# A place table made anew for a fused attention and feed-forward kernel

## The chip, the cores and the metric

The kernel runs on one core of one Trainium2 chip. The metric is the device time of one execution in microseconds; of several executions the median counts. The five engines of the core run side by side, each through its own list of instructions in a fixed order: TensorE (PE, with weight loads shown as PEld), VectorE (DVE), ScalarE (ACT), GpSimd (POOL) and SyncE (SP, which issues nearly all DMA transfers here). They meet only at semaphores.

## The reference

```python
q_n, k_n, c_n = (t / (norm(t) + 1e-06) for t in (q, k, centroids))     # q, k, v: 4 x 8 x 768 x 64
q_assign = argmax(q_n @ c_n.T); k_assign = argmax(k_n @ c_n.T)           # one of 16 clusters
mask = q_assign[..., :, None] == k_assign[..., None, :]
scores = where(mask, q @ k.T / sqrt(64), -1e9)
attn = exp(scores - max(scores)); attn = attn / (sum(attn) + 1e-9)
x = (attn @ v).transpose(0, 2, 1, 3).reshape(3072, 512)
h = x @ w_in                                                              # 512 x 2048
g = h * tanh(softplus(h))
out = g @ w_out                                                           # 2048 x 512
```

## The kernel before

There are 32 heads (4 batches of 8). A head's 768 query rows make three units of 256 rows, 96 units in all, and each unit has two halves of 128 rows. A half goes through: `scores` (four fp32 matrix products, lines 622 and 627, the second pair adding the cluster mask), `rowmax` (DVE, line 637), `expo` (ACT, line 651), a reciprocal of the row sums, `p_hi` and `p_lo` (lines 695 and 706, the split of the weights into two fp16 parts), a transposing DMA (line 736), and `pv` (lines 778 and 785). The first 24 units, the heads of batch 0, go another way: fp32 transposes on PE (`turn`, line 712), copies back on ACT (`back_t`, line 728) and fp32 products (line 759).

When a batch's heads are done, its feed-forward part begins, in 24 blocks of 256 rows by 256 columns of the hidden layer for each batch: `m1` (lines 856 to 858), `e_mish` (ACT, line 866), `e_gh` (POOL, line 870), `e_gl` (DVE, line 878), `m2` (lines 897 to 899), `m_out` and `m_store`. So `m1` and `m2` of one batch lie between the attention of the next.

Ahead of this stand preparations. Every weight tile is loaded as 64-bit words (`w_load`) and turned into fp32 by `w_abs` (ACT, line 262), `w_f32` and `w_or` (DVE, lines 270 and 277). Every head's operands A, B, T and Z are made from the loaded q and k (`prep_sc`, `prep_hi`, `prep_lo`, lines 444 to 461) and by copies between halves of the partitions (`copy_t`, `copy_z`, `copy_a`, `copy_b`, lines 467 to 473; a DMA for the most part, an ACT or DVE copy for some heads). `hot_copy` puts the rows with the cluster marks into Z and T by four small DMAs (lines 612 and 613). `warm` is a group of eight small matmuls without use for the result (line 289).

Each such step is a function, and the table `PLAN` gives every call of every function a place, 0 to 3682. The steps are issued in the order of their places, and so each engine's list is the order of places cut down to that engine's instructions:

```python
    def run(self):
        for op in sorted(self.ops, key=lambda op: self.ops[op][0]):
            self.issue(op)
```

The scores lie in PSUM buffers with the tag S, of which there are two; a buffer is free again when the exponential (`expo`) that reads it is done. So a half's scores can start only when the exponential of an earlier half has run. The blocks of `m1` have two PSUM buffers as well (tag H), freed by `e_mish`. All DMAs here stand in SP's one list, where an instruction that waits holds up all behind it.

Of the kernel before, what the change touches and what calls it, by code (L numbers as in the profile page):

```python
# [971 lines left out]
def spread(*axes):  # L972
    return list(itertools.product(*axes))


def places(args, text):
# [5 lines left out]
        0 1 2 3 4 5 6 15 18 19 20 67 68 69 92 93 94 95 96 97 116 117 240 241  # L982
# [20 lines left out]
        13 29 124 102 242 400 614 531 798 714 926 1116 1148 1276 1500 1360 1723 1727 1867 1792 2024 2090 2190 2314 2487  # L1003
        2426 2576 2716 2881 2963 3005 3131
    """),
    'assign_mm': places(spread((0, 1)), """
        14 55
    """),
    'prep_sc': places(spread(range(0, 32)), """
        16 56 158 215 454 602 675 818 899 715 1130 1246 1149 1322 1521 1361 1724 1728 1868 1793 2161 2091 2191 2315 2488  # L1010
        2427 2577 2717 2882 2964 3006 3132
    """),
    'prep_hi': places(spread(range(0, 32)), """
        17 57 194 342 455 603 676 819 900 1028 1131 1247 1336 1437 1575 1655 1775 1869 2016 2067 2177 2273 2376 2492
        2570 2670 2784 2878 3021 3090 3185 3276
    """),
    'w_load': places(spread(range(0, 32)), """
        22 21 26 37 28 40 31 134 44 51 112 135 132 173 161 235 80 98 47 36 146 175 238 298 234 255 299 319 330 340 387
        420
    """),  # L1020
    'w_abs': places(spread(range(0, 32)), """
        23 25 27 62 30 99 41 166 74 119 144 216 176 217 219 272 125 126 159 160 182 237 305 327 316 317 359 360 410 411
        439 472
    """),
    'w_f32': places(spread(range(0, 32)), """
        24 81 65 88 48 100 72 178 108 120 163 232 230 254 253 293 147 127 226 294 208 257 306 350 334 336 395 375 461
        418 440 473
    """),
    'v_load': places(spread(range(0, 4), range(0, 4)), """
        45 32 34 35 225 452 156 655 1084 1157 1546 1502 1900 1981 2332 2365  # L1030
    """),
    'copy_t': places(spread(range(0, 32)), """
        33 59 195 358 456 632 741 822 973 1045 1132 1260 1337 1438 1576 1656 1776 1883 2017 2070 2197 2276 2441 2512
        2600 2696 2785 2895 3024 3091 3186 3292
    """),
    'prep_lo': places(spread(range(0, 32)), """
        38 58 213 372 457 604 677 820 924 1029 1158 1248 1369 1457 1584 1665 1782 1870 2019 2068 2178 2274 2431 2493
        2571 2671 2827 2893 3022 3107 3196 3277
    """),
    'copy_a': places(spread(range(0, 32)), """  # L1040
        39 60 271 437 567 636 779 887 1025 1064 1159 1283 1370 1501 1585 1722 1848 1948 2061 2110 2198 2284 2442 2565
        2601 2743 2836 2977 3077 3155 3250 3375
    """),
    'assign_hot': places(spread((0, 1)), """
        42 66
    """),
    'assign_first': places(spread((0, 1)), """
        43 75
    """),
    'w_or': places(spread(range(0, 32)), """  # L1050
        46 82 79 89 49 101 150 218 109 121 169 286 288 263 278 333 148 145 227 296 209 258 307 351 335 341 396 409 462
        419 441 500
    """),
    'assign_put': places(spread((0, 1)), """
        50 76
    """),
    'copy_z': places(spread(range(0, 32)), """
        52 83 214 373 545 624 678 821 925 1044 1173 1249 1390 1458 1600 1666 1790 1886 2049 2069 2208 2275 2458 2494
        2649 2730 2828 2894 3030 3108 3227 3291
    """),  # L1060
    'rows_z': places(spread((0, 1)), """
        53 84
    """),
    'rows_t': places(spread((0, 1)), """
        54 85
    """),
    'hot_copy': places(spread(range(0, 32)), """
        61 86 262 450 592 633 742 895 1030 1046 1174 1261 1391 1459 1601 1670 1791 1887 2050 2071 2236 2277 2459 2513
        2650 2731 2889 2896 3031 3109 3228 3293
    """),  # L1070
    'copy_b': places(spread(range(0, 32)), """
        63 162 279 436 546 649 780 823 974 1047 1229 1321 1456 1517 1664 1743 1812 1936 2055 2094 2209 2327 2476 2529
        2659 2751 2862 2929 3034 3122 3262 3301
    """),
    'scores': places(spread(range(0, 96), (0, 1)), """
# [9 lines left out]
    """),  # L1085
    'rowmax': places(spread(range(0, 96), (0, 1)), """
# [9 lines left out]
    """),  # L1096
    'expo': places(spread(range(0, 96), (0, 1)), """
# [9 lines left out]
    """),  # L1107
    'turn': places(spread(range(0, 24), (0, 1), (0, 1)), """
# [4 lines left out]
    """),  # L1113
    'back_t': places(spread(range(0, 24), (0, 1), (0, 1)), """
# [4 lines left out]
    """),  # L1119
    'v_sq': places(spread(range(0, 4), range(0, 4)), """  # L1120
        103 104 105 106 528 896 613 811 1123 1237 1603 1696 1937 2095 2353 2555
# [237 lines left out]
```

## Time and profile before

| | us |
|---|---|
| three runs | 886.0, 886.37, 889.4 |
| median | 886.37 |
| profiled execution, its own time | 885.66 |
| span in its trace, first to last instruction | 883.9 |
| PE busy in the span | 850.3 |
| ACT busy | 659.3 |
| DVE busy | 614.4 |
| POOL busy | 235.3 |

The profiled execution took 885.66 us, 1.8 us more than its span, and lies 0.7 us below the median of the runs. TensorE had a granted clock of 0.96 in the first 40 us and of 1.00 from there on. Busy time is the union of the engine's instructions; PE's instructions overlap in the record, so that busy PE time holds the small stalls between matmuls too.

### The profile page before, as it was taken

What the parts mean: (1) busy time and instruction counts of PE and PEld (TensorE: products, weight loads), DVE (VectorE), ACT (ScalarE), POOL (GpSimd) and SP (SyncE); (2) the same over time, 40 slices, a digit from 0 to 9 for tenths busy, and PEclk for the clock granted to TensorE, in tenths of its full rate; (3) what the DMA queues carried; (4) which work ended last, traced back from release to release, by engine and by line L of the source; (5) the groups of instructions that cost most, each with busy time, mean ns of one, the idle gap of its engine ahead of it and who ended that gap; (6) DMA issues with size and microseconds to landing.
All of it is one profiled execution on the core that took longest, in us unless ns stands there. A gap on an engine that the chain in (4) does not pass through costs nothing. (4 is left out here: it accounts for less than half of the span.)

```text
span 883.9 us, 16511 instructions
## 1 busy us (share of the span) xinstructions
PE 850.3 (96%) x6271; PEld 608.5 (69%) x6271; DVE 614.4 (70%) x1080; ACT 659.3 (75%) x1058; POOL 235.3 (27%) x371
## 2 busy tenths in 40 slices
PE   7789999999999999999999999999999999999998
PEld 6667676687676676777676765777765765867673
DVE  8999889977767678967867778777767676311120
ACT  5778688899897999789998998788987896411120
POOL 2203454322313323212222413331321312311110
PEclk9999999999999999999999999999999999999999
DMA  9977332467669687977668588966577668300000
GB/s 341 327 231 215 82 105 57 108 122 145 126 118 172 107 175 156 175 149 152 127 110 172 120 162 161 156 126 129 114 129 155 121 124 143 70 13 13 13 13 24
DMA packets 252542, 116.19 MB, mean 131 GB/s; under 512 B 230640, under 2 KB 232816, under 8 KB 252464
## 3 DMA queue, kind: packets, MB, share of 16 engines
q1 hardware_dynamic: 252320, 115.02, 59.8%
q8 instruction: 49, 0.80, 0.4%
q14 instruction: 29, 0.24, 0.1%
q10 hardware_dynamic: 144, 0.13, 0.0%
HBM read 35.68 MB, written 6.29 MB: 47 GB/s over the span
## 5 line engine op out<-in xcount | busy, mean ns | idle before, releaser
L856 PE MATMUL h<-x,w 128*128 128x256 f16 x768 | 209.8, 273 | 3.4 <-ACT u L866 3.1
L651 ACT ACTIVATE p<-s,m 128x768 f32<-128x768 f32 x192 | 172.8, 901 | 52.0 <-DVE m L637 34.3
L858 PE MATMUL h<-x,w 128*128 128x256 f16 x768 | 209.3, 273 | 0.0
L857 PE MATMUL h<-x,w 128*128 128x256 f16 x768 | 209.3, 273 | 0.0
L637 DVE TENSOR_REDUCE m<-s 128x1 f32<-128x768 f32 x192 | 180.7, 948 | 24.2 <-PE s L627 23.4
L706 DVE SCALAR_TENSOR_TENSOR hl<-p,l,hl 128x768 f16<-128x768 f32 x142 | 147.2, 1041 | 61.5 <-ACT hl L695 58.6
L897 PE MATMUL O<-w,g 128*128 128x512 f16 x384 | 146.1, 381 | 0.1
L899 PE MATMUL O<-w,g 128*128 128x512 f16 x384 | 145.5, 379 | 0.0
L898 PE MATMUL O<-w,g 128*128 128x512 f16 x384 | 145.5, 379 | 0.0
L695 ACT ACTIVATE hl<-p,l 128x768 f16<-128x768 f32 x142 | 130.2, 929 | 18.0 <-ACT p L651 9.2
L878 DVE SCALAR_TENSOR_TENSOR g<-u,mscg,g 128x512 f16<-128x512 f32 x96 | 73.6, 777 | 87.9 <-POOL g L870 87.6
L622 PE MATMUL s<-A,B 128*128 128x384 f32 x384 | 117.5, 387 | 14.8 <-ACT p L651 10.7
L870 POOL TENSOR_SCALAR g<-u,mscg 128x512 f16<-128x512 f32 x96 | 70.5, 739 | 221.3 <-ACT u L866 186.1
L866 ACT ACTIVATE u<-h,msch 128x512 f32<-128x512 f32 x96 | 64.0, 685 | 66.2 <-PE h L858 49.0
L92 ACT ACT_TABLE_LOAD x78 | 100.1, 1283 | 2.1 <-PEq L1349 0.7
L627 PE MATMUL s<-Z,T 80*128 80x384 f32 x384 | 99.5, 340 | 0.0
L856 PEld LDWEIGHTS <-w 128*128 128x128 f16 x768 | 75.1, 98 | 21.1 <-issue 10.3
L622 PEld LDWEIGHTS s<-A,B 128*128 128x128 f32 x384 | 62.0, 190 | 39.3 <-ACT p L651 24.3
L663 POOL TENSOR_SCALAR l<-l 128x1 f32<-128x1 f32 x90 | 25.1, 279 | 233.4 <-ACT p L651 231.6
L857 PEld LDWEIGHTS <-w 128*128 128x128 f16 x768 | 75.2, 98 | 14.8 <-issue 4.1
L858 PEld LDWEIGHTS <-w 128*128 128x128 f16 x768 | 75.1, 98 | 8.7
L627 PEld LDWEIGHTS s<-Z,T 80*128 80x128 f32 x384 | 70.2, 190 | 0.0
(204 smaller groups left out, 1120.0 us busy)
## 6 DMA issues: line engine op xcount, KB each, us to landing
qk<-in_qk_dram SPq DMA_DIRECT2D x32, 384.0 KB, 4.0
stage<-in_w_in_dram SPq DMA_DIRECT2D x16, 512.0 KB, 7.6
stage<-in_w_out_dram SPq DMA_DIRECT2D x16, 512.0 KB, 4.5
vraw<-in_vP_dram SPq DMA_DIRECT2D x16, 384.0 KB, 4.5
out_dram<-osb SPq DMA_DIRECT2D x23, 256.0 KB, 2.7
A<-A SPq DMA_DIRECT2D x27, 192.0 KB, 3.1
Z<-B SPq DMA_DIRECT2D x18, 192.0 KB, 3.5
B<-T SPq DMA_DIRECT2D x18, 192.0 KB, 3.3
```

What stands on the lines that cost most here:

```text
L622: nc.tensor.matmul(s[:, j, :384], st["B", n][:, q0 : q0 + P], st["A", n][:, j * 384 : (j + 1) * 384], start=True, stop=False,)
L627: nc.tensor.matmul(s[:, j, :384], st["T", n][: D + NCL, q0 : q0 + P], st["Z", n][: D + NCL, j * 384 : (j + 1) * 384], start=False, stop=True,)
L637: nc.vector.tensor_reduce(m, st["s", i, a][:, :, :384], axis=AX.XY, op=ALU.max, negate=True)
L651: nc.scalar.activation(p.rearrange("p (n x) -> p n x", n=2), st["s", i, a][:, :, :384], AF.Exp, bias=st["m", i, a], scale=1.0, accum_out=l,)
L695: nc.scalar.activation(t[:, 0], p, AF.Copy, scale=r)
L706: nc.vector.scalar_tensor_tensor(t[:, 1], p, r, t[:, 0], op0=ALU.mult, op1=ALU.subtract)
L856: nc.tensor.matmul(o, wh, xh, start=(c == 0), stop=False)
L857: nc.tensor.matmul(o, wh, xl, start=False, stop=False)
L858: nc.tensor.matmul(o, wl, xh, start=False, stop=(c == 3))
L897: nc.tensor.matmul(o, gh, wh, start=(f == 0 and fi == 0), stop=False)
L898: nc.tensor.matmul(o, gh, wl, start=False, stop=False)
L899: nc.tensor.matmul(o, gl, wh, start=False, stop=(f == 7 and fi == 1))
```

## The change

Only the numbers in `PLAN` differ. The program's functions, the constants in `T` and the number of instructions on each engine are the same (PE 6001, DVE 1080, ACT 855, POOL 366 and SP 438 calls of instructions in both). The table was made by a planner that now counts with other durations of the first transfers and of the scores.

```diff
     'warm': places(spread(range(0, 24)), """
-        0 1 2 3 4 5 6 15 18 19 20 67 68 69 92 93 94 95 96 97 116 117 240 241
+        0 1 2 3 4 5 6 17 18 19 20 51 52 116 117 118 119 120 121 122 123 124 131 291
```

The order of units, blocks and heads is by and large the old one. What moves is mostly the neighbourhood: which of two steps of one engine goes first.

Place one, DVE in the first microseconds, from the step behind the centroids on. w are weight tiles (L270 is `w_f32`, L277 `w_or`), B, Z and T operands of heads 0 and 1, D, Dm and onehot the cluster assignment of a head, m0_0 the row maximum of unit 0. In the kernel before:

```order
37 L270 TENSOR_SCALAR w1_292<-w1_292 128x512
38 L461 SCALAR_TENSOR_TENSOR B_0_320<-qk0_244,scq_151,A_0_261 128x768
39 L559 TENSOR_REDUCE Dm0_328<-as0_246 128x12
...
44 L277 SCALAR_TENSOR_TENSOR w1_292<-stage0_289,w1_292 128x512
45 L270 TENSOR_SCALAR w3_304<-w3_304 128x512
46 L277 SCALAR_TENSOR_TENSOR w3_304<-stage4_300,w3_304 128x512
47 L469 CAST Z_0_349<-B_0_320 64x768
48 L590 CAST Z_0_349<-oh0_343 16x3x128 x2
49 L469 CAST B_0_320<-T_0_310 64x768
50 L270 TENSOR_SCALAR w2_298<-w2_298 128x512
51 L559 TENSOR_REDUCE Dm1_379<-as1_355 128x12
53 L637 TENSOR_REDUCE m0_0_406<-s0_0_372 128x1
```

And in the changed kernel:

```order
37 L461 SCALAR_TENSOR_TENSOR B_0_282<-qk0_244,scq_151,A_0_246 128x768
38 L270 TENSOR_SCALAR w1_287<-w1_287 128x512
39 L277 SCALAR_TENSOR_TENSOR w1_287<-stage0_284,w1_287 128x512
40 L469 CAST Z_0_291<-B_0_282 64x768
41 L270 TENSOR_SCALAR w1_287<-w1_287 128x512
42 L559 TENSOR_REDUCE Dm0_314<-as0_306 128x12
...
48 L270 TENSOR_SCALAR w3_303<-w3_303 128x512
49 L277 SCALAR_TENSOR_TENSOR w3_303<-stage4_301,w3_303 128x512
50 L277 SCALAR_TENSOR_TENSOR w1_287<-stage1_294,w1_287 128x512
51 L590 CAST Z_0_291<-oh0_361 16x3x128 x2
52 L469 CAST B_0_282<-T_0_248 64x768
53 L559 TENSOR_REDUCE Dm1_394<-as1_375 128x12
55 L637 TENSOR_REDUCE m0_0_404<-s0_0_388 128x1
```

Head 0's assignment (L559) now comes behind four more instructions, and two more weight steps (the second L270 and L277 on stage 1) stand ahead of the first row maximum. On PE the four `warm` groups that stood behind the assignment's matmuls now stand ahead of them.

Place two, ACT between the exponentials (L651) of units 41 and 42. hl are the fp16 weights of `p_hi` (L695), xf outputs of `pv` (L800), u the Mish of a block (L866). Before:

```order
357 L453 ACTIVATE A_15_4104<-qk15_3217,scq_151 128x768
358 L471 CAST T_15_4106<-A_15_4104 64x768
359 L471 CAST B_14_3873<-T_14_3858 64x768
360 L800 ACTIVATE xf1_2_2_4144<-o19_4114 64x256
361 L651 ACTIVATE p41_1_4162,l41_1_4163<-s41_1_4095,m41_1_4150 128x768
362 L92 ACT_TABLE_LOAD
363 L866 ACTIVATE u19_4192<-h19_4167,msch0_1342 128x512
```

And in the changed kernel:

```order
357 L453 ACTIVATE A_15_4051<-qk15_3258,scq_151 128x768
358 L471 CAST T_15_4053<-A_15_4051 64x768
359 L471 CAST B_14_3866<-T_14_3852 64x768
360 L800 ACTIVATE xf1_2_2_4148<-o19_4123 64x256
361 L800 ACTIVATE xf1_2_0_3979<-o19_4123 64x256
362 L695 ACTIVATE hl40_1_4154<-p40_1_4044,l40_1_4045 128x768
363 L651 ACTIVATE p41_1_4156,l41_1_4157<-s41_1_4110,m41_1_4150 128x768
364 L92 ACT_TABLE_LOAD
```

The exponential of unit 41, second half, now stands behind one more L800 and behind the L695 of unit 40, second half, which stood ahead of L453 before. On PE, at the same place, a group of six `m2` matmuls (block 13 of g, half 1) that stood ahead of the scores of unit 42 now stands behind them.

Place three, SP at the cluster rows of head 20 (Z_20 and T_20), which the scores of unit 60 read. pt are transposes of the fp16 weights hl. Before:

```order
263 L736 DMA_TRANSPOSE pt57_5831<-hl57_0_5780 128x12x128
264 L612 DMA Z_20_5777<-stg20_5868 16x384
265 L613 DMA T_20_5724<-stg20_5868 16x384
266 L612 DMA Z_20_5777<-stg20_5868 16x384
267 L613 DMA T_20_5724<-stg20_5868 16x384
268 L736 DMA_TRANSPOSE pt57_5831<-hl57_1_5890 128x12x128
```

And in the changed kernel:

```order
263 L736 DMA_TRANSPOSE pt57_5822<-hl57_0_5776 128x12x128
264 L736 DMA_TRANSPOSE pt57_5822<-hl57_1_5884 128x12x128
265 L612 DMA Z_20_5769<-stg20_5958 16x384
266 L613 DMA T_20_5736<-stg20_5958 16x384
267 L612 DMA Z_20_5769<-stg20_5958 16x384
268 L613 DMA T_20_5736<-stg20_5958 16x384
```

The four small copies have moved behind the transposing DMA of unit 57, second half. Beside these places, on ACT the exponential of unit 38, second half, has moved ahead of the preparation of head 14's A and T. On PE the step that stands just ahead of a half's four score matmuls is another one in many places. Among the 137 halves from unit 28 on these are, before and now: `m1` 40 and 55, `m2` 38 and 34, other scores 32 and 29, all others (`pv`, assignment, a transpose of the value scale) 27 and 19.

## Rows read from the trace of the kernel before

**Rows 1.** The page's first lines: the span, and PE's busy time, share and instructions.

```profile
span 883.9 us, 16511 instructions
PE 850.3 (96%) x6271; PEld 608.5 (69%) x6271; DVE 614.4 (70%) x1080; ACT 659.3 (75%) x1058; POOL 235.3 (27%) x371
```

**Rows 2.** Busy time of each engine in stretches of the span (start:end, length, then busy us and instructions of PE, PEld, DVE, ACT and POOL, the granted clock, the DMA share and GB/s).

```profile
20.00:90.00 70.00, 60.58 (x568) 47.73 (x567) 67.93 (x132) 53.61 (x113) 15.18 (x15) 0.99 0.81 261
90.00:180.00 90.00, 84.13 (x638) 62.55 (x634) 80.94 (x135) 74.13 (x158) 41.80 (x46) 1.00 0.36 87
180.00:760.00 580.00, 571.36 (x4111) 405.19 (x4109) 429.58 (x731) 501.67 (x743) 153.44 (x258) 1.00 0.72 140
760.00:884.00 124.00, 119.79 (x820) 79.31 (x818) 20.22 (x27) 20.16 (x31) 18.77 (x27) 1.00 0.06 19
```

**Rows 3.** What PE waited for between 180 and 760 us: us in total, times, longest.

```profile
PE s L622 <- ACT p L651: 4.5, 7, 1.2
PE h L856 <- ACT u L866: 3.1, 3, 1.6
PE vs3p L208 <- DVE vs3m L201: 0.3, 1, 0.3
```

**Rows 4.** What DVE waited for between 88 and 196 us, the first line: us in total, times, longest.

```profile
DVE m L637 <- PE s L627: 4.4, 7, 1.1
```

**Rows 5.** DVE's instructions in order of time, 8 to 21 us (start, length, instruction; in brackets idle time before it and what ended it).

```profile
8.57 0.28 DVE L196 COPY C<-ct 64x128 f32<-64x128 f32 x1
8.78 0.41 DVE L270 TENSOR_SCALAR w<-w 128x512 uint32<-128x512 uint32 x1
9.11 1.00 DVE L461 SCALAR_TENSOR_TENSOR B<-qk,scq,A 128x768 fp32r<-128x768 f32 x1
10.55 0.36 DVE L559 TENSOR_REDUCE Dm<-as 128x12 f32<-128x192 f32 x1 [0.44 <-PE as L545]
...
12.39 0.69 DVE L277 SCALAR_TENSOR_TENSOR w<-stage,w 128x512 uint32<-128x512 uint32 x1
...
14.16 0.56 DVE L469 CAST Z<-B 64x768 fp32r<-64x768 f32 x1
14.74 1.12 DVE L590 CAST Z<-oh 16x384 fp32r<-16x384 bf16 x2
15.89 0.93 DVE L469 CAST B<-T 64x768 fp32r<-64x768 f32 x1
16.85 1.94 DVE L270 TENSOR_SCALAR w<-w 128x512 uint32<-128x512 uint32 x1
...
19.48 0.95 DVE L637 TENSOR_REDUCE m<-s 128x1 f32<-128x768 f32 x1
```

**Rows 6.** PE in order of time in the same stretch: the assignment's matmuls, 32 matmuls of four `warm` groups, and the first scores.

```profile
8.91 1.60 PE L545 MATMUL as<-C,qk 128*128 128x128 f32 x12 [0.68 <-DVE C L196]
10.35 1.95 PE L289 MATMUL gram<-identb 128*128 128x128 bf16 x32
...
16.97 0.58 PE L622 MATMUL s<-A,B 128*128 128x384 f32 x2 [2.69 <-DVE B L469]
17.39 0.51 PE L627 MATMUL s<-Z,T 80*128 80x384 f32 x2
```

**Rows 7.** POOL in order of time, 14 to 19 us: the preparation of head 1.

```profile
14.37 1.12 POOL L444 TENSOR_SCALAR qk<-qk,scq 128x768 f32<-128x768 f32 x1 [8.92 <-PE as L545]
15.58 0.83 POOL L451 TENSOR_SCALAR A<-qk 128x768 fp32r<-128x768 f32 x1
16.49 2.01 POOL L459 TENSOR_TENSOR B<-qk,A 128x768 fp32r<-128x768 f32 x1
```

**Rows 8.** PE in order of time at three halves' scores: behind `m1` (line 858), behind `m2` (line 899), and behind other scores.

```profile
666.77 0.59 PE L622 MATMUL s<-A,B 128*128 128x384 f32 x2
667.20 0.51 PE L627 MATMUL s<-Z,T 80*128 80x384 f32 x2
...
465.87 0.70 PE L622 MATMUL s<-A,B 128*128 128x384 f32 x2
466.40 0.52 PE L627 MATMUL s<-Z,T 80*128 80x384 f32 x2
...
311.81 0.52 PE L622 MATMUL s<-A,B 128*128 128x384 f32 x2
312.16 0.52 PE L627 MATMUL s<-Z,T 80*128 80x384 f32 x2
```

**Rows 9.** PE in order of time: the scores of unit 40, first half, with their wait.

```profile
289.35 0.61 PE L622 MATMUL s<-A,B 128*128 128x384 f32 x2 [0.25 <-ACT p L651]
```

**Rows 10.** ACT in order of time, 304 to 311 us: the work ahead of the exponential of unit 41, second half (309.76).

```profile
305.04 1.76 ACT L695 ACTIVATE hl<-p,l 128x768 f16<-128x768 f32 x2 [0.56 <-ACT p L651]
...
309.36 0.38 ACT L800 ACTIVATE xf<-o 64x256 f32<-64x256 f32 x1
309.76 0.90 ACT L651 ACTIVATE p<-s,m 128x768 f32<-128x768 f32 x1
```

**Rows 11.** PE in order of time, 307 to 309 us: the first and the last of a group of six `m2` matmuls, and the `m1` matmul behind them.

```profile
307.19 0.39 PE L897 MATMUL O<-w,g 128*128 128x512 f16 x1
...
308.28 0.38 PE L899 MATMUL O<-w,g 128*128 128x512 f16 x1
...
308.82 0.27 PE L856 MATMUL h<-x,w 128*128 128x256 f16 x1
```

**Rows 12.** The instructions of lines 270 and 277 on DVE: shortest, median and longest in ns, first and last start.

```profile
L270 DVE TENSOR_SCALAR w<-w x32: 384/419/1935, 8.8 to 81.3; 128x512 uint32<-128x512 uint32 x32
L277 DVE SCALAR_TENSOR_TENSOR w<-stage,w x32: 661/692/1280, 12.4 to 85.2; 128x512 uint32<-128x512 uint32 x32
```

**Rows 13.** SP in order of time, 443 to 448 us: the first of the four copies of head 20's cluster rows, the last, and the transposing DMA of unit 57, second half.

```profile
443.26 0.90 SPq L612 DMA_DIRECT2D Z<-stg  x1
...
445.47 0.59 SPq L613 DMA_DIRECT2D T<-stg  x1
447.67 1.44 SPq L736 DMA_TRANSPOSE pt<-hl  x1
```

**Rows 14.** PE in order of time: the scores of unit 60, first half; and of the DMAs by line in 430 to 460 us the copies of cluster rows (KB each, median us from issue to landing).

```profile
455.00 0.70 PE L622 MATMUL s<-A,B 128*128 128x384 f32 x2
...
Z<-stg SPq DMA_DIRECT2D x4, 24.0 KB, 2.1
```

**Rows 15.** What SP waited for in the whole span, the first line: us in total, times, longest.

```profile
SPq L736 <- DVE hl L706: 116.1, 49, 7.7
```

More of the change, by code (lines that the diff above doesn't have):

```diff
@@ L1002 @@
     'qk_load': places(spread(range(0, 32)), """
-        13 29 124 102 242 400 614 531 798 714 926 1116 1148 1276 1500 1360 1723 1727 1867 1792 2024 2090 2190 2314 2487
-        2426 2576 2716 2881 2963 3005 3131
+        13 38 93 125 241 374 594 474 807 679 909 1050 1162 1264 1495 1388 1712 1723 1885 1815 2018 2119 2178 2316 2488
+        2424 2586 2714 2862 2942 2990 3122
+    """),
+    'prep_sc': places(spread(range(0, 32)), """
+        14 62 195 333 441 573 675 812 900 680 1079 1247 1163 1293 1518 1389 1713 1724 1886 1816 2180 2120 2179 2317 2489
+        2425 2587 2715 2863 2943 2991 3123
@@ new lines @@
+    """),
+    'prep_hi': places(spread(range(0, 32)), """
+        15 63 196 334 442 574 676 813 901 1033 1132 1248 1336 1442 1577 1644 1773 1860 2012 2068 2181 2274 2426 2490
+        2567 2673 2773 2883 3015 3104 3185 3284
+    """),
+    'copy_t': places(spread(range(0, 32)), """
+        16 81 228 335 445 598 739 815 977 1048 1133 1258 1337 1443 1578 1645 1774 1862 2013 2071 2198 2277 2435 2502
+        2604 2722 2774 2897 3020 3107 3186 3287
+    """),
+    'prep_lo': places(spread(range(0, 32)), """
+        21 64 203 369 454 575 677 814 924 1046 1155 1249 1372 1451 1586 1664 1778 1861 2027 2069 2182 2275 2431 2491
+        2568 2674 2828 2895 3016 3105 3194 3285
@@ new lines @@
+    """),
+    'w_load': places(spread(range(0, 32)), """
+        22 28 30 39 32 59 40 140 44 75 136 213 174 152 198 248 58 60 141 114 166 156 249 297 231 258 298 312 313 330 373
+        393
+    """),
+    'w_abs': places(spread(range(0, 32)), """
+        23 29 31 50 33 97 69 172 94 111 137 214 204 205 201 301 107 108 167 233 189 240 303 327 292 311 354 355 401 402
+        430 461
+    """),
+    'w_f32': places(spread(range(0, 32)), """
+        24 34 42 74 46 98 89 173 95 112 157 242 229 283 212 302 129 109 238 288 210 259 304 357 336 344 379 366 447 416
+        431 462
@@ new lines @@
+    """),
+    'w_or': places(spread(range(0, 32)), """
+        25 48 78 84 47 99 138 230 96 113 158 279 281 284 286 328 146 150 239 299 211 260 305 358 337 345 380 406 448 417
+        432 491
+    """),
+    'copy_z': places(spread(range(0, 32)), """
+        26 77 227 370 565 597 678 817 925 1047 1165 1257 1386 1452 1594 1665 1800 1889 2050 2070 2203 2276 2447 2492
+        2652 2721 2842 2896 3033 3106 3228 3286
+    """),
+    'copy_a': places(spread(range(0, 32)), """
+        27 115 289 436 490 610 751 816 1013 1074 1156 1288 1373 1522 1587 1717 1838 1942 2045 2094 2199 2328 2436 2571
+        2606 2738 2835 2968 3079 3157 3276 3376
@@ L1005 @@
     """),
     'assign_mm': places(spread((0, 1)), """
[L1007 removed]
+        35 61
     """),
[L1009 to L1011 removed]
+    'assign_hot': places(spread((0, 1)), """
+        36 67
     """),
[L1013 to L1015 removed]
@@ L1016 @@
[L1016 to L1027, printed above, removed]
+    'assign_first': places(spread((0, 1)), """
+        37 76
@@ L1028 @@
     """),
     'v_load': places(spread(range(0, 4), range(0, 4)), """
-        45 32 34 35 225 452 156 655 1084 1157 1546 1502 1900 1981 2332 2365
+        41 49 43 45 215 649 489 656 1123 1129 1530 1394 1896 1996 2359 2365
     """),
[L1032 to L1052, printed above, removed]
+    'w_sq': places(spread(range(0, 32)), """
+        53 90 91 155 224 225 226 275 276 277 278 280 282 285 287 342 383 384 385 386 387 388 389 390 391 392 469 470 502
+        503 518 579
@@ L1122 @@
     """),
     'v_sum': places(spread(range(0, 4)), """
-        107 897 1717 2556
+        106 895 1720 2558
     """),
     'v_turn': places(spread(range(0, 4)), """
-        110 954 1718 2557
+        134 961 1721 2559
     """),
     'v_top': places(spread(range(0, 4)), """
-        111 955 1719 2558
+        135 962 1722 2560
     """),
-    'p_hi': places(spread(range(0, 96), (0, 1)), """
[9 rows of a table removed]
+    'pair_mm': places(spread(range(2, 31, 2)), """
+        151 440 668 897 1113 1308 1559 1758 1918 2154 2372 2551 2768 2978 3170
@@ L1191 @@
-    """),
-    'p_lo': places(spread(range(0, 96), (0, 1)), """
[9 rows of a table removed]
[9 rows of a table added]
     """),
     'invert_pair': places(spread(range(0, 12)), """
-        203 339 427 547 611 605 744 842 915 990 1052 1119
+        190 329 425 543 606 643 746 837 914 995 1058 1115
+    """),
+    'pair_first': places(spread(range(2, 31, 2)), """
+        199 457 674 926 1149 1347 1584 1776 1950 2195 2409 2553 2788 2984 3172
     """),
     'pv': places(spread(range(0, 48), range(0, 3)), """
[7 rows of a table removed]
-    """),
-    'pair_first': places(spread(range(2, 31, 2)), """
-        205 470 674 929 1150 1346 1577 1778 1952 2188 2380 2580 2786 2986 3176
[7 rows of a table added]
@@ L1217 @@
     """),
     'pair_turn': places(spread(range(2, 31, 2)), """
-        206 538 739 930 1151 1347 1578 1779 1953 2189 2389 2581 2787 3028 3198
+        209 534 737 927 1150 1348 1585 1777 1951 2196 2410 2611 2789 3031 3202
     """),
     'v_split': places(spread(range(0, 4), range(0, 4)), """
-        370 368 467 239 1002 1015 1034 1067 1834 1894 1876 1855 2695 2651 2869 2760
+        253 449 648 371 998 1011 1036 1065 1832 1887 1871 1845 2685 2643 2879 2766
+    """),
+    'v_low': places(spread(range(0, 4), range(0, 4)), """
+        254 505 860 496 999 1012 1037 1066 1833 1888 1872 1853 2750 2688 2880 2848
@@ L1223 @@
+    """),
+    'pv_scale': places(spread(range(0, 96)), """
[5 rows of a table added]
     """),
     'pair_put': places(spread(range(2, 31, 2)), """
-        261 539 740 978 1172 1348 1599 1781 2048 2235 2421 2603 2863 3029 3226
-    """),
-    'pv_scale': places(spread(range(0, 96)), """
[5 rows of a table removed]
+        267 535 738 989 1173 1349 1610 1799 2049 2259 2432 2648 2860 3032 3227
     """),
     'pv_out': places(spread(range(0, 96)), """
[5 rows of a table removed]
[5 rows of a table added]
+    """),
+    'w_sum': places(spread((0, 1)), """
+        343 580
     """),
     'x_out': places(spread(range(0, 96)), """
[5 rows of a table removed]
[5 rows of a table added]
```

67 lines of the change are left out of this document (27 added, 40 removed), and 280 rows, old and new, of the table PLAN.

## The prediction

> **What bounds the kernel now.** I read the page's first lines, then the windows, then the waits, and only then single stretches. The page gives PE 96% of the span and DVE 70% [rows 1]; that is a mean over two unlike parts, which the windows take apart [rows 2]. From 20 to 90 us DVE is busy 67.93 of 70 us and PE 60.58: DVE sets the pace, since beside the attention of batch 0 it turns the weights into fp32. From 90 to 180 us DVE has still 80.94 of 90. From 180 to 760 us PE has 571.36 of 580, and from 760 to the end 119.79 of 124. So up to about 180 us a microsecond of DVE is a microsecond of the kernel, and behind it one of PE is. A new order can win what the bounding engine now waits. PE's waits in the long part come to 4.5 us on exponentials, 3.1 us on the Mish and 0.3 us on the value scale, 7.9 us together [rows 3]; the bigger idle sums of ACT, POOL and SP cost nothing by themselves. DVE's largest wait around the first part's end is 4.4 us for scores, in seven pieces [rows 4]. That is what a new table has to work with: some 12 us of 884. What it can lose has no such limit.
>
> **The sum** is made against the profiled execution, 885.66 us (a span of 883.9 and 1.8 around it); the median of the runs, 886.37, is 0.7 above it, and I add that at the end.
>
> **1. The start, on DVE.** Before, the centroids' last copy ends at 8.85 us (8.57 + 0.28), DVE loses 0.44 waiting for the assignment's matmuls, and the first row maximum ends at 20.43 (19.48 + 0.95) [rows 5]. Now PE does the four warm groups first (1.95, of which 0.68 fits in its wait for C), then the assignment (1.60) [rows 6]: 8.91 − 0.68 + 1.95 + 1.60 ≈ 11.8. DVE has from 8.85 on B (1.00), L270 (0.42), L277 (0.69), the Z copy (0.56) and another L270 (0.42), together to 11.94, so the 0.44 goes. Five assignment instructions take 1.93 as before (10.55 to 12.48 in start and end): 13.87. Two L270 and two L277, 2 × 0.42 + 2 × 0.69: 16.1. The one-hot casts (1.12): 17.2. Next is the copy of B out of T. In the kernel before, the L270 that met POOL's third preparation step (16.49, 2.01 long, end 18.50 [rows 7]) took 1.94 instead of 0.42 and ended 18.79, 0.29 behind that step. I take it that the copy meets the same fate: it starts at 18.5, ends at 19.1. Two assignment instructions take it to 19.8, but the scores come later: before, they ended 1.08 behind the B copy (16.82 to 17.90 [rows 5, 6]), so 20.2, and the row maximum ends at 21.15. That is 0.72 later than before with one L270 and one L277 more behind it (1.11): a gain of 0.4. Bounds: if nothing is held up by POOL, the copy starts at 17.2 and 1.3 more is won, −1.7; if POOL's steps are themselves held up by DVE's (rival C), +1.3. I take **−0.4**, since its main term, a DVE instruction stretched by that very POOL step, stands in a row.
>
> **2. PE, what stands ahead of the scores.** From the first score matmul to the second pair it takes 0.43 us behind m1 (666.77 to 667.20), 0.53 behind m2 (465.87 to 466.40) and 0.35 behind other scores (311.81 to 312.16) [rows 8]. The counts change by m1 +15, m2 −4, scores −3 and the rest −8. That is 15 × 0.43 − 4 × 0.53 − 3 × 0.35 = +3.28, less eight of the rest, which no row here prices: between 0.43 and 0.53 each, 3.44 to 4.24. Bounds −0.16 and −0.96; I take the middle, **−0.5**.
>
> **3. A wait that goes.** The scores of unit 40, first half, waited 0.25 for an exponential [rows 9]. It is that of unit 38, second half, which now runs ahead of head 14's preparation on ACT: **−0.25**. What was hidden then is that preparation, due only for units 42 and later.
>
> **4. A wait that comes.** Before, ACT did an L695 pair (from 305.04, 1.76 for two), later an L800 (309.36, 0.38) and at 309.76 the exponential of unit 41, second half, 0.90 long, end 310.66 [rows 10]. Now one L695 (0.88) and one L800 (0.38) more stand ahead of it in the neighbourhood; the L695 stood ahead of L453 before, behind a wait of 0.56, so that what is new is between nothing and 0.9. PE comes to the scores that need this buffer at 311.81 before [rows 8], and now earlier, since a group of six m2 matmuls has moved behind them. Six such matmuls start 0.22 us apart (307.19 to 308.28 for the first and the last [rows 11]), 1.3 us for the group; so PE arrives at 310.5 and finds the buffer free between 310.7 and 311.6 plus the release. The price lies between 0 and 1.2; I take **+0.9**, the upper half, because everything queued on PE behind those scores waits with them, and ACT has no gap there to catch up in.
>
> The other places that I followed (the blocks' Mish, the value scales, the late exponentials) have the same releaser in both orders, so I leave their waits as they are: of the 7.9 us, all but 0.25 stays. In the last 124 us PE has next to no idle time to win or to lose [rows 2].
>
> −0.4 − 0.5 − 0.25 + 0.9 = −0.25. That gives 885.4 for a profiled execution, and with the 0.7 to the median **886.1 us**: no change. By the bounds the likeliest case lies between −1.7 − 0.96 − 0.25 + 0 = −2.9 and +1.3 − 0.16 − 0 + 1.2 = +2.3, that is 883.5 to 888.7 as a median. About 0.5% (4.4 us) is what a measurement of this kernel can tell from no change.
>
> **Rivals.**
>
> A is the sum above.
>
> B, faster. The order as a whole is better fitted to real durations: half of PE's 7.9 us between 180 and 760 us goes (−3.9) [rows 3], and half of DVE's 4.4 (−2.2) [rows 4]. 886.1 − 6.1 = 880.0. For it: exponentials move ahead of preparations in more than one place, and 4.5 of the 7.9 are waits for exponentials. Against it: at most of these waits the instructions ahead of the releaser are the same ones in both orders.
>
> C, a little slower from the start. L270 runs in 384 to 1935 ns with a median of 419, L277 up to 1280 with 692 [rows 12], so POOL and DVE hold each other up in this kernel. If in the new order DVE's second L270 and its two L277 (0.42 + 2 × 0.69 = 1.80) come in first and hold POOL's three steps, the third ends at 20.3, not 18.5; the B copy at 20.86, the scores at 21.94, the row maximum at 22.9, which against 20.43 + 1.11 is +1.3. It replaces −0.4: 887.8. It decides if the L270 starts before POOL's first step does; by the sum it is at 13.87, and that step at 14.37 [rows 7]. Against: before, two L277 beside no POOL step cost 0.69 each, and POOL may come earlier than DVE. The Trainium skill ("SBUF — State Buffer", section "Who interferes with whom") says that a DVE copy, cast or tensor_scalar in a two-port mode and a GpSimd instruction shut each other out for the whole instruction, whoever comes first. By that rule this rival holds, and the trace agrees for L270 beside POOL's third step (1.94 for 0.42).
>
> D, slower. SP's list is in order, and the four copies of head 20's cluster rows now stand behind the transposing DMA of unit 57, second half. Before, they issued from 443.26 to 446.06 (2.80 for four), and that transpose at 447.67 for 1.44 [rows 13]. Now the first copy issues at 449.1, the last at 451.3, and with 2.1 to land it is there at about 453.4 to 454.0; PE wants the rows at 455.00 for unit 60 [rows 14]. The cover is 1 us. The transpose waits for p_lo, as SP does 49 times in the span, for 116.1 us together, at longest 7.7 [rows 15]. If p_lo is late by that once, the rows land at 461.7, and PE stands for 6.7 with all its list behind it: 886.1 + 6.7 = 892.8. It decides from a lateness of 1 us on. For it: p_lo stands in DVE's list among other work, and DVE has 429.58 of 580 us there [rows 2], so that it queues at times. Against: DVE's order there is nearly the old one, and 7.7 is the worst of 49.
>
> **How the numbers follow.** A has .55, B .23, C .06, D .16. A and C lie within 0.5% of 886.37 (882.0 to 890.8); B with a part of A's tail is faster by more, .23; D with other lists that come late in the same way is slower by more, .20; the rest, .57, is no change. The range from 880.0 to 892.8 leaves out half of B and somewhat under half of D, .18 together.
>
> **What the profile after would show.** Step 1: no wait on L559 behind the centroids, the copy of B beginning where POOL's third step ends, and the first row maximum ending near 21.2; a POOL step longer than 2.01 speaks for C. Step 2: fewer microseconds in busy PE between 180 and 760 us by about half a one. Step 3: no wait before the scores of unit 40. Step 4: a wait of 0.6 to 1.2 for an exponential at unit 42's scores. D: a wait of PE on a DMA ahead of the scores of unit 60; B: PE's waits for exponentials and Mish under 4 us, and DVE's for scores under half. I am wrong if PE's waits between 180 and 760 us change by over 4 us either way, or if the first part, up to the point where PE takes over, is longer or shorter by as much.

## The result, and the profile after

The changed kernel takes 896.66 us (median of seven runs, 892.79 to 900.01), beside 887.32 for the kernel before on the same chip: 1.0097 times as long, with an interval from 1.0079 to 1.0115. Run a second time among the experiments it took 894.48 us, 1.0095 (1.0074 to 1.0117). The forecast was 886.1 us and no change, with a range up to 892.8; the kernel is slower, by 0.8 to 1.2%, and lies outside that range.

The profiled execution took 893.48 us, with a span of 891.5 us; it is one of the faster ones, 3.2 us below the median. First the page's lines, then the windows (stretch and length, then busy us of PE, PEld, DVE, ACT and POOL, then the granted clock), then PE's waits from 180 to 760 us. They answer to [rows 1], [rows 2] and [rows 3].

```profile
span 891.5 us, 16505 instructions
PE 852.8 (96%) x6271; PEld 608.2 (68%) x6271; DVE 613.7 (69%) x1080; ACT 658.0 (74%) x1058; POOL 238.3 (27%) x371
```

```profile
20.00:90.00 70.00, 60.49 (x535) 48.31 (x536) 63.16 (x117) 51.28 (x108) 14.81 (x15) 0.93 0.80 251
90.00:180.00 90.00, 84.95 (x645) 62.37 (x645) 81.47 (x141) 73.37 (x159) 45.14 (x45) 1.00 0.36 91
180.00:760.00 580.00, 566.52 (x4062) 399.01 (x4060) 430.36 (x729) 498.80 (x741) 152.83 (x258) 1.00 0.71 139
```

```profile
PE s L622 <- ACT p L651: 10.5, 13, 1.5
PE O L897 <- ACT osb L907: 1.2, 2, 1.0
PE h L856 <- ACT u L866: 0.7, 2, 0.5
PE o L778 <- DVE xf L819: 0.6, 1, 0.6
PE s L622 <- DVE D L509: 0.2, 1, 0.2
```

The page's shares hardly differ. The loss shows in the two stretches that each have one bounding engine. Between 20 and 90 us DVE, which was busy 67.93 us, is busy 63.16, and the granted clock is 0.93. Between 180 and 760 us PE is busy 566.52 us where it was 571.36; its waits have grown from 7.9 to 13.2 us. Scores that wait for an exponential alone grew by 6.0 (4.5 to 10.5 us, 7 to 13 times), and those of `m1` for the Mish shrank (3.1 to 0.7).

**The start.** PE in order of time in the changed kernel:

```profile
20.42 0.50 PE L580 MATMUL oh<-identb,onehot 128*128 128x128 bf16 x3 [2.12 <-DVE onehot L573]
...
23.60 2.76 PE L352 MATMUL gram<-vraw 128*128 128x128 bf16 x24
28.09 4.18 PE L289 MATMUL gram<-identb 128*128 128x128 bf16 x72 [1.73 <-DVE vs0q L310]
32.08 0.60 PE L622 MATMUL s<-A,B 128*128 128x384 f32 x2
```

DVE at the same place (the row maximum that needs those scores):

```profile
33.08 0.96 DVE L637 TENSOR_REDUCE m<-s 128x1 f32<-128x768 f32 x1 [3.23 <-PE s L627]
```

The 72 matmuls of line 289 are nine `warm` groups. They write into the tile `gram`, which `v_sq` (line 352) fills as well, so behind `v_sq` they wait until DVE has read it (line 310), and then take 4.18 us. The scores of unit 1, first half, stand behind them in PE's list, and DVE, which had no wait of this kind in the kernel before, loses 3.23 us. In the kernel before, PE in order of time at the same place:

```profile
23.10 2.86 PE L289 MATMUL gram<-identb 128*128 128x128 bf16 x48
25.79 1.54 PE L352 MATMUL gram<-vraw 128*128 128x128 bf16 x24
29.97 0.27 PE L208 MATMUL vs0p<-ident,vs0m 128*1 128x128 f32 x1 [2.63 <-DVE vs0m L312]
30.08 1.05 PE L289 MATMUL gram<-identb 128*128 128x128 bf16 x16
30.94 0.60 PE L622 MATMUL s<-A,B 128*128 128x384 f32 x2
```

There only two groups stood between `v_sq` and those scores. Six more stood ahead of `v_sq`, where they did not have to wait for DVE, and behind which PE waited 2.63 us anyway.

**Behind 180 us.** One of the new waits in full: ACT, then DVE, then PE in the changed kernel, in order of time. Line 800 is `pv_scale`, first of unit 51 and then of unit 50; line 819 is `pv_out`, DVE's addition, which reads the same PSUM tile.

```profile
417.73 0.38 ACT L800 ACTIVATE xf<-o 64x256 f32<-64x256 f32 x1
420.37 0.38 ACT L800 ACTIVATE xf<-o 64x256 f32<-64x256 f32 x1 [2.25 <-DVE xf L819]
420.77 0.90 ACT L651 ACTIVATE p<-s,m 128x768 f32<-128x768 f32 x1
```

```profile
417.94 0.96 DVE L637 TENSOR_REDUCE m<-s 128x1 f32<-128x768 f32 x1 [0.71 <-PE s L627]
418.81 1.01 DVE L706 SCALAR_TENSOR_TENSOR hl<-p,l,hl 128x768 f16<-128x768 f32 x1
419.85 0.42 DVE L819 SCALAR_TENSOR_TENSOR xf<-o,xf 64x256 f32<-64x256 f32 x1
```

```profile
421.82 0.61 PE L622 MATMUL s<-A,B 128*128 128x384 f32 x2 [1.28 <-ACT p L651]
```

The second `pv_scale` waits for the addition of its partner (the two share one tile), DVE has a row maximum and a `p_lo` ahead of that addition, and the exponential of unit 54 stands behind the waiting instruction. PE, at the next scores, pays 1.28 us. In the kernel before, the first `pv_scale` stood ahead of a table load and an exponential, and the second waited 0.22. Over the whole span ACT's waits of this kind (line 800 for DVE: us, times) went from the first line to the second:

```profile
  DVE xf L819: 6.6, 7
```

```profile
  DVE xf L819: 15.9, 16
```

### The profile page after: what moved, and what is told of

The parts are those of the page before. It is cut to its first block, busy times and chain, and to the rows that moved or that the text cites. A ratio compares the mean times of both kernels' runs of the same rounds, so it can differ in the third digit from the quotient of the medians.

```text
span 891.5 us, 16505 instructions
## 1 busy us (share of the span) xinstructions
PE 852.8 (96%) x6271; PEld 608.2 (68%) x6271; DVE 613.7 (69%) x1080; ACT 658.0 (74%) x1058; POOL 238.3 (27%) x371
## 5 line engine op out<-in xcount | busy, mean ns | idle before, releaser
L651 ACT ACTIVATE p<-s,m 128x768 f32<-128x768 f32 x192 | 172.5, 900 | 49.8 <-DVE m L637 33.2
L695 ACT ACTIVATE hl<-p,l 128x768 f16<-128x768 f32 x142 | 129.7, 929 | 17.8 <-ACT p L651 7.7
L870 POOL TENSOR_SCALAR g<-u,mscg 128x512 f16<-128x512 f32 x96 | 72.7, 762 | 229.4 <-ACT u L866 193.0
L866 ACT ACTIVATE u<-h,msch 128x512 f32<-128x512 f32 x96 | 64.1, 686 | 60.2 <-PE h L858 40.0
```

The costliest lines, as they stand in the source:

```text
L651: nc.scalar.activation(p.rearrange("p (n x) -> p n x", n=2), st["s", i, a][:, :, :384], AF.Exp, bias=st["m", i, a], scale=1.0, accum_out=l,)
L695: nc.scalar.activation(t[:, 0], p, AF.Copy, scale=r)
```

## The experiments

Two theories stood at the beginning. S: the loss arises at the start, by the nine warm groups and a lower clock. L: it arises behind 107 us, by `pv_scale` steps that stand nearer each other. All ratios are to the kernel before, measured together with the run. In the diffs a line is a stretch of the table, in the order of places, of the engine named.

**Old start, new rest, and the complement.** Both tables hold nearly the same steps up to place 660 (about 107 us), so that a table can be cut there.

```diff
-places 0 to 659: as in the new table
+places 0 to 659: as in the old table
 the rest: as in the new table
```

> The first 660 places (to about 107 us) in the old order, the rest in the new one. Theory S (the loss arises at the start: nine warm groups ahead of a score, and the lowered clock that follows from PE's idle time there): back near the kernel before, 887 to 889 us, and clock as before. Theory L (the loss arises after 180 us, where pv_scale steps stand nearer each other on ACT and hold exponentials): 891 to 893 us, PE's waits between 180 and 760 us still 13 us instead of 7.9. The trace of the changed kernel suggests about 2.4 us for S and 5.4 us for L, so I expect 892.

Measured: 893.54 us, 1.0076 (1.0056 to 1.0095). The complement, the new start with the old rest:

> The complement: the first 660 places in the new order, the rest in the old one. Theory S alone: 893 to 897 us, like the changed kernel, with a low clock in part of the runs. Theory L alone: 886 to 888 us. With both, 889 to 892 us, and PE's waits between 180 and 760 us near 7.9 us.

Measured: 891.05 us, 1.0044 (1.0025 to 1.0063). PE's waits for exponentials between 180 and 760 us, in the first and in the second of the two:

```profile
PE s L622 <- ACT p L651: 10.7, 13, 1.7
```

```profile
PE s L622 <- ACT p L651: 4.5, 8, 1.2
```

Both theories hold a part: 6.4 us (893.54 − 887.17) come from the order behind 107 us, 3.9 (891.05 − 887.17) from that ahead of it. Their sum of 10.3 lies a little above the 9.3 and 7.9 us of the two measurements of the changed kernel and agrees with both within the intervals.

**The nine warm groups moved.** Three runs. In the changed kernel they go just behind the scores that waited for them (PE):

```diff
-warm(13) ... warm(21)  scores(1,0)
+scores(1,0)  warm(13) ... warm(21)
```

> The changed kernel, with the nine warm groups that stand ahead of the scores of unit 1, first half, moved just behind them. Theory S by the warm groups: the row maximum of unit 1, first half, comes at about 28 us and not at 33.1, DVE's wait of 3.2 us there goes, and 2 to 3 us of the total with it. Rival (the wait is only moved: the next scores, of unit 2, then stand behind the same 4 us of warm matmuls): DVE loses about as much ahead of the next row maximum and the total is within 1 us of the changed kernel.

Measured: 892.55 us, 1.0069 (1.005 to 1.0088). The rival was partly right: the wait was cut but moved. What DVE waited for between 15 and 92 us (us, times, longest):

```profile
DVE vs0m L374 <- PE vs0p L208: 2.1, 1, 2.1
DVE m L637 <- PE s L627: 1.2, 2, 0.8
```

Now it is the transpose of the value scale (line 208) that stands behind the warm matmuls. So they have to go farther. In the next two runs the start is the new one and the rest the old; in one, all nine stand behind the scores of unit 2, second half, in the other, four of them fill PE's idle time behind the scores of unit 0 first:

```diff
-warm(13) ... warm(21)  scores(1,0) ... scores(2,1)
+scores(1,0) ... scores(2,1)  warm(13) ... warm(21)
```

```diff
-scores(0,1)  assign_put(1) ... warm(13) ... warm(21)  scores(1,0) ... scores(2,1)
+scores(0,1)  warm(13) ... warm(16)  assign_put(1) ... scores(1,0) ... scores(2,1)  warm(17) ... warm(21)
```

> As the run with four groups in the gap, but all nine warm groups stand behind the scores of unit 2, second half, and PE's idle time at 18 to 20 us stays empty. Theory S with the clock: the clock in 20 to 25 us stays near 0.5, v_sq takes twice its time there, DVE waits 1 to 3 us more than in the run with four groups in the gap and the total is 1 to 3 us above it. If only the place ahead of the scores counts (rival), both runs are within 1 us.

> New start, old order from 107 us on (891.05 us in its own run), with the nine warm groups that stood ahead of the scores of unit 1, first half, moved: four into PE's idle time behind the scores of unit 0, second half, at about 18 us, five behind the scores of unit 2, second half. Theory S with the clock: the granted clock in 20 to 25 us rises from 0.50 to above 0.8, DVE's waits between 15 and 92 us fall from 6 to 3 us or less, and the total comes to 886.5 to 888. Without the clock's part (rival): the clock there stays near 0.5 and the total is that of the run with all nine moved late.

Measured: 886.77 us, 1.0 (0.9988 to 1.0011), with all nine late; 886.82 us, 0.9995 (0.9985 to 1.0006), with four in the gap. To within 1 us, the new start costs nothing without the warm groups ahead of those scores: its 3.9 us are theirs, with what a low clock adds to them. DVE's waits between 15 and 92 us, 5.0 us with the nine groups in place, came to 2.4 with all nine late and 3.3 with four in the gap. The clock's part, as I had put it, fell: the two runs differ by 0.05 us. The windows tell why. The column ahead of the last two is the granted clock; first the run with all nine late, then that with four in the gap:

```profile
20.00:25.00 5.00, 4.16 (x28) 4.00 (x29) 4.78 (x10) 2.29 (x4) 0.00 (x0) 0.50 1.04 398
25.00:30.00 5.00, 3.10 (x33) 2.40 (x31) 4.84 (x11) 4.93 (x10) 0.00 (x0) 0.99 1.04 398
30.00:35.00 5.00, 3.62 (x29) 2.54 (x30) 4.90 (x12) 4.56 (x10) 0.90 (x1) 1.00 0.73 235
```

```profile
20.00:25.00 5.00, 3.66 (x50) 3.27 (x47) 4.81 (x9) 2.31 (x4) 0.00 (x0) 1.00 1.04 398
25.00:30.00 5.00, 2.76 (x15) 2.45 (x16) 4.84 (x11) 4.92 (x10) 0.00 (x0) 0.61 1.04 394
30.00:35.00 5.00, 4.71 (x21) 2.75 (x20) 4.24 (x8) 4.39 (x9) 0.00 (x0) 0.50 0.68 224
```

In the profile with warm matmuls in the gap the clock stays up from 20 to 25 us and falls behind PE's next idle time instead. So these two runs do not show what a start without a low clock would take; the low stretch only moved. DVE, which sets the pace here, is busy 4.2 to 4.9 us of each 5 in both.

**Pairs of `pv_scale`.** In the changed kernel four exponentials go ahead of the `pv_scale` step that held them (ACT alone), as here:

```diff
-pv_scale(51)  pv_scale(50)  expo(54,1)
+pv_scale(51)  expo(54,1)  pv_scale(50)
```

> The changed kernel, with four exponentials on ACT moved ahead of the pv_scale step that waits for DVE's addition of its partner (units 54, 58, 68 and 84); no other engine's order changes. Theory L by the pairs of pv_scale: the waits of PE at about 421.8 (1.28), 452.5 (1.10), 545.7 (1.13) and 670.9 us (1.30) go or shrink below 0.3 each, PE's waits between 180 and 760 us fall from 13 to about 9, and the total falls by 3 to 4 us. Rival (ACT or DVE is late there anyway): the waits stay within 0.3 of what they are or move a few us on, and the total stays within 1 us.

Measured: 891.48 us, 1.0054 (1.0034 to 1.0074), against 894.48 to 896.66 for the changed kernel, which was not measured together with it. The waits at 421.8, 452.5 and 670.9 us shrank or went; that for the exponential of unit 69 at 545 us stayed at 1.16. All of PE's waits came to 10.3 us, where I had expected about 9; those for exponentials:

```profile
PE s L622 <- ACT p L651: 7.4, 11, 1.6
```

Then the theory as a whole, from both sides. In the kernel before, ten pairs are brought as close as in the new table; in the changed kernel, the close pairs (17, where the expectation counts 16) are taken apart by moving one or two of the next steps of ACT ahead of the second:

```diff
-pv_scale(65)  copy_t(24)  pair_put(24)  p_hi(68,0)  pv_scale(64)
+pv_scale(65)  pv_scale(64)  copy_t(24)  pair_put(24)  p_hi(68,0)
```

```diff
-pv_scale(65)  pv_scale(64)  expo(68,1)  copy_t(24)
+pv_scale(65)  expo(68,1)  copy_t(24)  pv_scale(64)
```

> The kernel before; only on ACT, in ten pairs of pv_scale steps that read one PSUM tile, the second step is moved up to where it stands in the changed kernel (next to the first, or one step behind it). Theory L (the second step of a pair waits for DVE's addition behind the first, and holds the exponentials behind it): ACT's waits on line 800 for DVE rise from 6.6 us to 13 or more, PE's waits for exponentials from 4.5 us by 3 to 5, total 889.5 to 892. Rival (the loss after 107 us comes from the other steps that changed neighbours: exponentials, p_hi, DVE's row maxima): PE's waits rise by less than 1 us, total within 1 us of the kernel before.

Measured: 887.31 us, 1.0008 (0.9995 to 1.0022); PE's waits went from 7.9 to 9.0 us. ACT's waits on line 800 for DVE stayed at 6.6 us in 7 places, where I had expected 13 or more. At units 51 and 50, ACT, then DVE's addition for unit 51:

```profile
413.50 0.79 ACT L800 ACTIVATE xf<-o 64x256 f32<-64x256 f32 x2
```

```profile
417.01 0.42 DVE L819 SCALAR_TENSOR_TENSOR xf<-o,xf 64x256 f32<-64x256 f32 x1
```

The second `pv_scale` follows the first at once and does not wait for the addition, which comes 2.7 us later. The move had put it ahead of `pv_out(51)` in the table; in the changed kernel these three stand at places 2121, 2122 and 2123, the addition in the middle. Nine of the ten pairs here have the second step ahead of the addition. So this run does not test theory L. It shows that the wait on the shared tile hangs on the order in the table: in the profiles of both kernels and of all experiments, every wait of line 800 for DVE is at a pair with the addition between its steps, and none at a pair without. Whether moving the second steps of the changed kernel ahead of the addition would win its loss back was not run.

> The changed kernel; only on ACT, in 16 close pairs of pv_scale steps the next one or two steps are moved ahead of the second, so that two stand between. Theory L: ACT's waits on line 800 for DVE fall from 15.9 us to below 6, PE's waits between 180 and 760 us from 13.2 to 7 or less, and the total by 5 to 7 us against the changed kernel in the same call. Rival as above: no more than the 3 us that the four moved exponentials gave.

Measured: 898.99 us, 1.0117 (1.0093 to 1.0142), beside 894.48 for the changed kernel measured together with it. ACT's waits on line 800 fell from 15.9 to 4.1 us as meant, but PE's only from 13.2 to 12.1. So theory L in this form fell with this run: the waits of close pairs are not the cause by themselves. Most of the 4.5 us by which the run is slower goes with the clock: at a mean granted clock of 0.992 it took 895.3 and 895.4 us and the changed kernel 894.4 and 894.5, while the other three of its five executions had 0.987. Lines of this run show what stands in their place at one wait. ACT, then DVE, at unit 69:

```profile
548.55 0.90 ACT L651 ACTIVATE p<-s,m 128x768 f32<-128x768 f32 x1 [2.94 <-DVE m L637]
```

```profile
545.13 0.75 DVE L878 SCALAR_TENSOR_TENSOR g<-u,mscg,g 128x512 f16<-128x512 f32 x1
...
545.87 0.54 DVE L525 TENSOR_REDUCE Dm<-D 128x24 f32<-128x384 f32 x1
...
547.54 0.92 DVE L637 TENSOR_REDUCE m<-s 128x1 f32<-128x768 f32 x1
```

With ACT freed, the exponential waits 2.94 us for a row maximum that stands on DVE behind `e_gl` of block 47 and `pair_turn` of head 24. In the kernel before, `pair_turn` of that head ran at 529.3 us and the row maximum at 536.1, with other work of DVE in between. The pair was one of two late things there.

That run also shows the start at its worst, in a stretch where its order is still that of the changed kernel: the same nine warm groups, at a clock of 0.53 between 30 and 35 us, take 7.02 us where they took 4.18, and DVE's wait behind them is 6.08. PE, then DVE:

```profile
28.75 7.02 PE L289 MATMUL gram<-identb 128*128 128x128 bf16 x72 [2.84 <-DVE vs0q L310]
```

```profile
36.57 0.96 DVE L637 TENSOR_REDUCE m<-s 128x1 f32<-128x768 f32 x1 [6.08 <-PE s L627]
```

**Place by place.** If it is not one kind of step, it may be a sum of places, each with what is late there. Old start and new rest, with eight steps moved, on ACT and DVE:

```diff
 (ACT) the four exponentials as above
-pv_scale(88) ... m_out(8,0)
+m_out(8,0)  pv_scale(88)
 (DVE)
-e_gl(47)  recip(68,1)  pair_turn(24)  rowmax(69,0)
+recip(68,1)  rowmax(69,0)  e_gl(47)  pair_turn(24)
-v_low(3,1) ... rowmax(72,0)  rowmax(72,1)
+rowmax(72,0)  rowmax(72,1)  v_low(3,1)
```

> Old start and new order from 107 us on (893.5 us in its own run), with eight steps moved: on ACT four exponentials ahead of the pv_scale step that waits (units 54, 58, 68, 84) and m_out of block group 8 ahead of the pv_scale step of unit 88; on DVE pair_turn of head 24 and e_gl of block 47 behind the row maximum of unit 69, and v_low of batch 3 behind those of unit 72. If the loss after 107 us is a sum of single places at which ACT or DVE now comes late, PE's waits at 421, 452, 545, 566, 670 and 743 us go or shrink below 0.4 each, PE's waits fall from 13 to 7 or 8 us, and the total to 888 or 889. Rival (PE meets the next late exponential a few us on, as in the run with the pairs taken apart): PE's waits stay above 10 us, total 891 or more.

Measured: 889.04 us, 1.003 (1.0011 to 1.0049), 2.1 us above the kernel before (886.93) measured with it: of the 6.4 us of the order behind 107 us, some 4.3 are gone. The profiled execution was the slowest of the twelve, 897.16 us, with low clock ahead of 180 us; PE's waits from 180 to 760 us in it, where the clock was 1.00:

```profile
PE s L622 <- ACT p L651: 5.6, 10, 1.6
PE h L856 <- ACT u L866: 1.5, 4, 0.6
PE h L857 <- POOL x L836: 0.5, 1, 0.5
PE h L856 <- POOL x L828: 0.5, 1, 0.5
```

The six places are below 0.5 us each, the one at 421 us at 0.32 and that at 566 us at 0.46; two waits of 0.5 for POOL are new. PE's waits came down to 9 us and not to 7 or 8, the expectation for the rival being above 10. The eight steps were not moved one by one. Of the remaining 2.1 us, 1.2 lie in PE's waits, 9.1 us beside 7.9 in the kernel before; the rest I have not taken apart.

**A version that beats both.** What held at these places was then used on the kernel before: an exponential ahead of a waiting `pv_scale`, two other steps ahead of another one, and, at the start, the `w_f32` step that took 1.94 us beside POOL [rows 5] behind the first row maximum.

```diff
 (ACT)
-pv_scale(80)  expo(84,0)
+expo(84,0)  pv_scale(80)
-pv_scale(84)  copy_t(31)  p_hi(88,1)
+copy_t(31)  p_hi(88,1)  pv_scale(84)
 (DVE)
-w_f32(2) ... rowmax(0,0)  w_f32(6)
+... rowmax(0,0)  w_f32(2)  w_f32(6)
```

> The kernel before with three places mended by what the runs so far showed: the exponential of unit 84, first half, ahead of the pv_scale step of unit 80; copy_t of head 31 and p_hi of unit 88, second half, ahead of the pv_scale step of unit 84; on DVE the w_f32 step that took 1.94 us beside POOL's third preparation step moved behind the first row maximum. By theory L PE's waits at 668.9 (1.21) and 710.7 us (1.57) go; by the row of that w_f32 step the start wins about 1 us. Together 3 us, 884 us. Rival (PE meets the next late exponential, DVE's copy takes over the stretching by POOL): 886 to 887.5 us.

Measured: 883.58 us, 0.9958 (0.9943 to 0.9974). PE's wait at 710.7 us went, that at 668.9 fell from 1.21 to 0.73, and its waits between 180 and 760 us came to 5.3 us. What each of the three steps gave was not measured by itself. The same two late places on the new start, with four warm groups in the gap and five late, and the old order from 107 us on:

> The run with four groups in the gap plus the two late places of the mended old kernel (the exponential of unit 84 and the steps ahead of the pv_scale step of unit 84). If the new start, freed of its warm groups, is as good as the old one with its w_f32 step moved, 883 to 884 us; if it keeps a loss of its own (DVE waits for weights at 70 to 80 us), 885 to 886.

Measured: 882.6 us, 0.9946 (0.9931 to 0.9961), the lowest of all, though its interval overlaps that of the run before it. PE's largest waits between 180 and 760 us:

```profile
PE s L622 <- ACT p L651: 3.9, 7, 1.1
PE h L856 <- ACT u L866: 0.9, 1, 0.9
```

## Why the prediction was wrong

The bounds were read rightly: DVE up to some 180 us, PE behind it, and what could be won was 12 us of waits. That losses have no such limit stood there too, but the sum took no account of it. The prediction's own sign of being wrong came: PE's waits between 180 and 760 us changed by 5.3 us, more than 4.

**Step 1, the start (−0.4): failed by what it left out.** Its own stretch came out better than said. The first row maximum ended at 18.52 us, not 21.15; some 0.9 of that is not the change's, since the centroids were done earlier (PE's `cent_turn` began at 7.02 us instead of 7.92, behind the same instructions: 30 warm matmuls ahead of it took 2.39 us instead of 3.40; in the second profile of the changed kernel it began at 7.74, and the row maximum ended at 19.47). Head 0's assignment stands behind three more instructions in DVE's list, not four, and the sum had them right. My main term, the B copy held up by POOL, did not occur; POOL was held up instead. DVE, then POOL, in the changed kernel:

```profile
14.85 1.12 DVE L590 CAST Z<-oh 16x384 fp32r<-16x384 bf16 x2
15.89 0.54 DVE L469 CAST B<-T 64x768 fp32r<-64x768 f32 x1
...
17.56 0.96 DVE L637 TENSOR_REDUCE m<-s 128x1 f32<-128x768 f32 x1 [0.35 <-PE s L627]
```

```profile
15.70 1.43 POOL L451 TENSOR_SCALAR A<-qk 128x768 fp32r<-128x768 f32 x1
```

POOL's second step took 1.43 us, where it took 0.83 before [rows 7], and the copy 0.54, where it took 0.93 [rows 5]: before, this copy had itself been held up, by POOL's second step, and I had not read that from its row. The Trainium skill ("SBUF — State Buffer", section "Who interferes with whom") says that whoever issues first has the shared port pair for the whole instruction. The kernel before agrees with that at the L270 of 1.94 us, which began 0.36 us behind POOL's third step. At the copy the rows do not show who was first: it begins behind POOL's second step in both kernels, by 0.31 us and by 0.19, and that step itself begins while a cast of line 590 is running; yet the outcome is the opposite. As rival C this price was put on the wrong side: up to 92 us no wait of PE or DVE is for a POOL step.

What cost 3.9 us stood in the first line of the diff: `warm` 116 to 124. I counted the four groups that moved ahead of the assignment and not the nine that moved together ahead of the scores of unit 1. In a part bounded by DVE I had followed DVE's list and, on PE, only the stretch up to the first scores. The runs with the nine moved late (886.77) and in place (891.05) show it. This is the first step that failed: a term of PE's list that the sum had left at nothing.

**Step 2 (−0.5): right in sign, and of its small size.** From the first matmul of a half's scores to the second pair, the 132 halves from 205 us on took 59.77 us together before and 59.48 after, worked out from the start times of the two traces: −0.3, within the bounds of −0.16 to −0.96.

**Step 3 (−0.25): right.** The scores of unit 40, first half, start at 291.89 us without a wait.

**Step 4 (+0.9): wrong.** There is no wait at unit 42, and the 0.9 came out as nothing. ACT, then PE:

```profile
312.19 0.90 ACT L651 ACTIVATE p<-s,m 128x768 f32<-128x768 f32 x1
```

```profile
313.24 0.60 PE L622 MATMUL s<-A,B 128*128 128x384 f32 x2
```

The exponential ends at 313.09 and PE comes at 313.24. The lower bound, nothing, was right; I had chosen from the upper half because ACT had no gap to catch up in, but it came to PE's time by a margin of 0.15.

**"The other places have the same releaser in both orders, so I leave their waits as they are": the second step that failed, and the larger one.** PE's waits between 180 and 760 us grew by 5.3 us, at some eight places. I compared which step releases a wait; what changed was what stands ahead of the releaser on its own engine and on the engine that it waits for in turn. At unit 54 that is three engines in a row: DVE's `pv_out` behind a row maximum and a `p_lo`, ACT's `pv_scale` behind that, the exponential behind this, PE at the end.

**The rivals.** B (half of the waits gone) was the opposite of what happened. D named a place that did not cost anything: head 20's copies went out at 455.89 to 458.03 us and PE took the scores of unit 60 at 461.80 without a wait. The first copy and the scores both came 6.8 us later than D had them, so that `p_lo` was not late against PE and the cover stayed. But its kind, a step that now stands behind one that waits, is what happened on ACT. It had a chance of 0.16 with other lists counted in; a table with some hundreds of moved neighbours at a bound engine deserved more.

## What to carry to other kernels

Where an order is made anew, count every step that moves on each engine near the bound, those without use for the result too: nine groups of idle work ahead of one score cost 3.9 us here. A wait is not kept by keeping its releaser: follow the list ahead of the releaser, and where an entry there waits for a third engine, that engine's list as well. A step moved across another that uses the same tile can gain or lose a wait by that alone. And where a bound engine waits some ten times for 1 us each, look for what is late at each place and move that one step; taking a whole kind of step apart (17 pairs) gained nothing, eight places chosen from the trace took back 4.3 of 6.4 us, and three others won 0.4% over the kernel before.

## What the runs showed of the hardware

The time of a run goes with its mean granted clock. Of the twelve runs of the changed kernel the four at a mean of 0.993 or more took 892.8 to 893.5 us, and the eight at 0.992 or less 894.4 to 900.0. In the profiles of the two kernels the low stretches lie in the first 50 us, the first of them behind idle time of PE: 0.84 between 20 and 25 us in the kernel before, 0.50 in the changed one, where PE had been busy 1.72 of the 5 us ahead. They are not bound to the start: in the run with eight steps moved, whose profiled execution took 897.16 us, the clock was 0.77 between 155 and 160 us, with PE busy 4.00 of the 5, and 0.54 in the next 5; in the run with the pairs apart it was 0.66 between 550 and 555 us, and PE had been busy 3.27 of the 5 us ahead. A mean of 0.5 is TensorE's lower level, 1.2 GHz. With 0.53 in 30 to 35 us the 72 warm matmuls took 7.02 us, with 1.00 there 4.18, so that idle work in front of needed work costs most just when the clock is low.
